# An mLSTM layer and a gated FFN in one kernel: the hand-written sequence of all steps laid anew

## Chip, core and metric

The kernel runs on one core of one Trainium2 chip. The metric is the device time of one execution in microseconds (us). Three timed executions of the kernel before took 588.6, 589.43 and 590.79 us; their median is 589.43 us. One further execution was profiled, and all rows below are from it.

## What is computed

The reference first runs an mLSTM over 4 batches, 8 heads and 768 steps with head size 40, all in float32: at each step a state matrix `C` and a vector `n` fade by a forget gate and take in a new key and value, and the query reads them. Then it runs a gated feed-forward network (FFN) over all 3072 tokens (320 features, 1536 hidden):

```python
C = f_stab * C + i_stab * outer(vt, kt)
n = f_stab * n + i_stab * kt
y[t] = sigmoid(o_gate[t]) * (C @ qt) / maximum(abs(n @ qt), 1)
...
gate = sigmoid(x @ w_gate)
val = x @ w_val
out = (gate * val) @ w_out
```

## The kernel before

**Tiling.** The sequence is cut into 6 chunks of 128 steps. A chunk `c` and a batch `b` make a *unit*, and the unit's number is 4c + b, so there are units 0 to 23, and units 8 to 23 are those of chunks 2 to 5. Within a unit the attention is done as masked matrix products; between chunks a state `cst` is carried for each batch. When the units of a chunk are done, their outputs (`xh`, `xl`: two float32r parts of each number, since the FFN multiplies in three passes for accuracy) go through the FFN in *tiles* numbered 0 to 102. A full tile is 512 tokens wide, a half tile 256; half tiles are 0 to 7, 16 to 45 (chunk 1 and the first of chunk 2) and 79 to 102 (chunk 5).

**The order.** Every piece of work is put into a table under a short key, and a string `ORDER` says in which sequence the pieces are issued. A word is a key, `*3` repeats it, and `/` flips which of two PSUM banks (`pa0`, `pa1`) the next attention tile takes. Each engine and each queue runs its own pieces in the sequence of the string and waits only where data or a buffer isn't ready. Nothing else orders the work:

```python
for word in ORDER.split():
    if word == "/":
        other("pa")
        continue
    key, _, n = word.partition("*")
    for _ in range(int(n or 1)):
        f, args = todo[key].pop(0)
        f(*args)
```

**The keys.** For tile n: `tn` is one matmul of the 16 of the up projection (line 865), `pn` one matmul of the down projection (line 903; 12 in a full tile, 6 in a half one), and `tan`, `tgn`, `thn`, `tln` the gate's steps between them on ACT (ScalarE), DVE (VectorE) and POOL (GpSimd) (lines 878 to 892). Weights are decoded under `w...` keys. For unit n: `ln` with a letter loads q, k, v or o (line 310), `ldn` the decay matrix (line 409).

For units 8 to 23 the queries and keys are *turned* (heads and time exchanged) by a detour through a scratch array in device memory, where units of even batches share `scr0` and those of odd ones `scr1`:

- `an.0` and `an.1` turn 32x32 blocks of q and of k on DVE (line 603); `ahn.x` rounds to float32r on ACT or DVE (line 607); `aln.x` makes the low part on POOL (line 612).
- `asn.0` to `asn.3` save q, `asn.4` to `asn.7` save k, in strips of 32 partitions, on SP's DMA queue (line 616).
- `sn`, four times, loads the turned k (twice: `ks`) and then the turned q (twice: `qs`) for the scores (line 650). There is one buffer each of `ks` and `qs` for all units, so `sn` waits for the scores of unit n - 1.
- `aqn`, three times, loads the turned q again as `qk`, for reading the carried state (line 623). There are two buffers of it.
- `cin` multiplies the carried state by `qk` (matmul `in`, line 714): the first piece on PE (TensorE) that needs `aqn`. `bn.g` are the scores (line 693) and need `sn`.

Further keys of unit n that stand below: `cn` gathers the values (64 small matmuls, line 663), `zn` makes the chunk's contribution to the state (line 818), `dn` transposes the output for the FFN (line 783), `bmn.g` masks the scores on DVE (line 699), `ohn` and `on` halve and store a finished block of 128 output rows (lines 917 to 923).

```python
for x, i in ((1, 0), (0, 1)):
    put(f"s{n}", take, x, i, True)
    put(f"s{n}", take, x, i, False)
...
for j in range(3):
    put(f"aq{n}", keep, j)
```

The first two chunks (units 0 to 7) turn q and k by transposes on PE instead and have no such detour.

Of the kernel before, what the change touches and what calls it, by code (L numbers as in the profile page):

```python
# [144 lines left out]
p32 tg33 th33 p32 t34*3 p32 t34*2 p32 t34 b10.2 bm10.2 t34*2 p33 e12a t34*2 tl33 ci10 cf10 t34*2 p33 t34 p33 t34
p33 z10 e12 ta34 t34 tg34 t35*2 c10 cs10 th34 s11*4 aq11*3 cv10 p33 t35 ld13 t35*2 p33 t35 p34 tl34 t35*3 lv14 cg10
t35 zd10.1 t35*2 p34 lk13 cv10 t35 zm10.0 t35*3 p34 ct12 / ci11 bk11 ta35 tg35 p34*3 t36*2 th35 t36*3 tl35 t36
zd11.0 t36 v14 t36*9 p35*6 cv10 ta36 tg36 t37 th36 t37*7 zm10.1 t37 tl36 t37*6 ta37 cf11 t37 p36*3 za10.1 tg37
# [982 lines left out]
```

## Time and profile before

| | before |
|---|---|
| median of 3 runs | 589.43 us |
| the profiled execution | 588.31 us |
| its span (first to last instruction) | 586.5 us |
| PE busy / weight loads | 526.6 us (90%) / 469.9 us (80%) |
| DVE, ACT, POOL busy | 318.1, 211.9, 175.2 us |
| mean granted TensorE clock | 0.965 of full speed |
| moved by DMA | 75.55 MB |

A profile's page has the busy time of each engine, the chain of work that ended last, and groups of instructions by source line. Views of the trace give the waits of an engine and what ended each, the instructions in order of time, and busy times in chosen stretches. Times in rows count from the first instruction. "SPq" is the issue of a DMA by SP. A clock of 1.00 is 2.4 GHz, one of 0.50 is 1.2 GHz.

### The profile page before, as it was taken

To read this page: it belongs to the slowest core of one execution; us is meant where nothing else is said; L and a number is where in the kernel's file an instruction comes from. 1 tells how busy PE (TensorE), PEld (TensorE's weight loads), DVE (VectorE), ACT (ScalarE), POOL (GpSimd) and SP (SyncE) were. 2 spreads that over 40 slices of the span, in tenths; PEclk is the share of its full clock that TensorE was granted. 3 is DMA by queue.
4 is the path that set the end of the run, shared out by engine and by line. 5 is a ranking of instruction groups with operands and counts; after the bars stand their busy time and mean duration, and the time that the engine had idled before them with its cause. 6 is when DMAs were issued, how large, how long until landed. Compare 5 with 4: busy or idle time off the path is not lost.

```text
span 586.5 us, 12196 instructions
## 1 busy us (share of the span) xinstructions
PE 526.6 (90%) x4667; PEld 469.9 (80%) x4667; DVE 318.1 (54%) x740; ACT 211.9 (36%) x548; POOL 175.2 (30%) x251
## 2 busy tenths in 40 slices
PE   8889999998599989499997848999958999999997
PEld 7668878887599988488886737888847788899997
DVE  5999989785167456036553412655613446443332
ACT  5697576524025422043422313332222242122221
POOL 5544224646223314124232213434121211202100
PEclk9999999999799999799997978999987999999999
DMA  9987792426959856638594545978674756100000
GB/s 233 271 221 193 200 216 60 108 65 129 194 106 194 176 119 115 148 67 164 136 195 99 122 94 91 203 157 161 132 156 76 177 99 131 52 22 24 12 12 23
DMA packets 227578, 75.55 MB, mean 129 GB/s; under 512 B 207040, under 2 KB 215424, under 8 KB 227520
## 3 DMA queue, kind: packets, MB, share of 16 engines
q1 hardware_dynamic: 226432, 74.51, 59.2%
q8 instruction: 37, 0.61, 0.5%
q10 hardware_dynamic: 1088, 0.26, 0.2%
q14 instruction: 21, 0.17, 0.1%
HBM read 57.61 MB, written 17.14 MB: 127 GB/s over the span
## 4 chain that ended last, share of the span: by engine, by line
PE 65%; issue 11%; DMA 8%; DVE 7%; POOL 5%; SPq 3%; ACT 2%; DVEq 0%; POOLq 0%; ACTq 0%
PE pg L865 36%; PE po L903 17%; DMA qk<-scr0q 3%; SPq L616 2%; PE in L714 2%; PE av L663 2%; PE s L693 2%; DMA ks<-scr0k 1%; PE cs L818 1%; PE xt L783 1%; PE s L688 1%; POOL d L422 1%; PE mb L985 1%; DMA qk<-scr1q 1%; DMA d<-mscr 1%
## 5 line engine op out<-in xcount | busy, mean ns | idle before, releaser
L878 ACT ACTIVATE sg<-pg 128x256 f32<-128x256 f32 (+1 forms) x103 | 48.3, 469 | 235.3 <-PE pg L865 214.4
L881 DVE SCALAR_TENSOR_TENSOR sg<-sg,pg 128x256 f32<-128x256 f32 (+1 forms) x103 | 54.0, 524 | 130.1 <-ACT sg L878 109.4
L865 PE MATMUL pg<-xh,wh 128*128 128x256 f32 (+1 forms) x412 | 113.4, 344 | 2.6 <-ACT sg L878 1.5
L865 PE MATMUL pg<-xl,wh 128*128 128x256 f32 (+1 forms) x412 | 110.2, 335 | 0.0
L865 PE MATMUL pg<-xh,wl 128*128 128x256 f32 (+1 forms) x412 | 109.9, 334 | 0.0
L903 PE MATMUL po<-oh,gh 128*128 128x320 f32 x288 | 90.9, 321 | 4.9 <-DVE gh L888 2.5
L903 PE MATMUL po<-ol,gh 128*128 128x320 f32 x288 | 92.2, 323 | 0.0
L903 PE MATMUL po<-oh,gl 128*128 128x320 f32 x288 | 91.0, 323 | 0.5 <-POOL gl L892 0.4
L892 POOL TENSOR_TENSOR gl<-sg,gh 128x256 fp32r<-128x256 f32 (+1 forms) x45 | 44.1, 980 | 157.3 <-ACT gh L886 89.4
L865 PEld LDWEIGHTS pg<-xh,wh 128*128 128x128 f32 x412 | 71.7, 193 | 10.5 <-ACT sg L878 5.2
L865 PEld LDWEIGHTS pg<-xh,wl 128*128 128x128 f32 x412 | 71.4, 192 | 5.2
L865 PEld LDWEIGHTS pg<-xl,wh 128*128 128x128 f32 x412 | 70.6, 192 | 5.7
L903 PEld LDWEIGHTS po<-oh,gh 128*128 128x128 f32 x288 | 54.5, 191 | 9.7 <-ACT gh L886 3.8
L865 PE MATMUL pg<-xl,w 128*128 128x256 f32 (+1 forms) x206 | 60.2, 336 | 0.0
L903 PEld LDWEIGHTS po<-oh,gl 128*128 128x128 f32 x288 | 55.1, 192 | 4.2 <-POOL gl L892 0.8
L903 PEld LDWEIGHTS po<-ol,gh 128*128 128x128 f32 x288 | 55.0, 191 | 2.3
L714 PE MATMUL in<-cst,qk 120*128 120x123 f32 (+1 forms) x120 | 19.8, 310 | 40.2 <-DMA qk<-scr0q 33.3
L865 PE MATMUL pg<-xh,w 128*128 128x256 f32 (+1 forms) x206 | 53.7, 331 | 0.0
L714 PEld LDWEIGHTS in<-cst,qk 120*128 120x128 f32 (+1 forms) x120 | 18.7, 224 | 42.6 <-issue 42.0
L699 DVE TENSOR_TENSOR d<-s,d 128x384 f32<-128x384 f32 (+1 forms) x66 | 33.1, 508 | 34.1 <-PE s L693 31.6
L886 ACT ACTIVATE gh<-sg 128x256 fp32r<-128x256 f32 (+1 forms) x61 | 31.1, 510 | 39.9 <-DVE sg L881 34.7
L417 ACT ACTIVATE d<-d,at 128x128 f32<-128x128 f32 x136 | 43.0, 393 | 6.6 <-DMA d<-mscr 6.6
(170 smaller groups left out, 779.9 us busy)
## 6 DMA issues: line engine op xcount, KB each, us to landing
d<-mscr SPq DMA_DIRECT2D x22, 512.0 KB
k<-in_k_dram SPq DMA_DIRECT2D x24, 160.0 KB
v<-in_v_dram SPq DMA_DIRECT2D x24, 160.0 KB
o<-in_o_gate_dram SPq DMA_DIRECT2D x24, 160.0 KB
st_o<-in_moe_w_out_dram SPq DMA_DIRECT2D x12, 320.0 KB
out_dram<-ob SPq DMA_DIRECT2D x24, 160.0 KB
scr0q<-qt SPq DMA_DIRECT2D x32, 120.0 KB
scr1q<-qt SPq DMA_DIRECT2D x32, 120.0 KB
```

Of the source, the lines that this page charges most:

```text
L417: nc.scalar.activation(d[:, h, :], d[:, h, :], AF.Exp, bias=at[:, c, b * H + h : b * H + h + 1], scale=-1.0)
L616: nc.sync.dma_start(dst.rearrange("(g c) r -> c g r", c=32), both[x][32 * i : 32 * i + 32].rearrange("c x (j r) -> c (x j) r", r=32).bitca ...
L663: nc.tensor.matmul(dst[xs], lhs[:, xs], rhs, start=True, stop=True)
L693: nc.tensor.matmul(ps[g][:, m, :], ks[: 3 * D, h0 + m, :], qs[: 3 * D, h0 + m, :], start=True, stop=True)
L699: nc.vector.tensor_tensor(x, ps[g][:, :nh, :], x, ALU.mult)
L714: nc.tensor.matmul(pi[:, h0 : h0 + nh, :], qk[u][:r, g, :], cst[:r, b, g, : nh * DA], start=True, stop=True)
L865: nc.tensor.matmul(pg[x], w[:, a, fs] if a < 2 else w[:, fs], y[c][:, a, n0:n1], start=first, stop=a == 2 and y is xl)
L878: nc.scalar.activation(sg[0], pg[0], AF.Tanh, scale=0.5)
L881: nc.vector.scalar_tensor_tensor(sg[0], sg[0], 1.0, pg[1], ALU.add, ALU.mult)
L886: nc.scalar.activation(gh[u][:, :nt], sg[0], AF.Copy)
L892: E('gl0' if c == 0 else 'gl', f'tl{n}').tensor_tensor(gl[u][:, :nt], sg[0], gh[u][:, :nt].bitcast(F32), ALU.subtract)
L903: nc.tensor.matmul(po[t], g[c, j, t0][:, (t - t0) * P : (t - t0 + 1) * P], o[:, j, :], start=j == 0 and first, stop=j == NF - 1 and last)
```

## The change

Only the string `ORDER` differs. Old and new string hold the same 4513 pieces; `/` stands 21 times in the old one and 36 times in the new one. So no instruction, size, engine or buffer differs, and each engine, SP's queue and POOL's included, runs the same pieces in another sequence. The old string issues the turning of a unit in blocks (`as8.0` to `as8.7` in one run, then `s8`, then `aq8`); the new one deals its pieces out singly, among those of other units. The cut shows the places of units 8, 16 and 20 in the old string, and of 8, 18 and 20 in the new one:

```diff
     'EU': 8,
 ORDER = """
...
-bm7.2 cv6 ta16 tg16 cr6 cx6 lk9 ci7 cf7 zd7.1 p15 c7 cs7 z7 e9a zm7.0 p15 oh0 o0 a8.0 a8.1 t17*3 zm7.1 t17 cv7
-t17*2 ah8.0 ah8.1 th16 tl16 t17 al8.0 al8.1 t17*4 cg7 p15 t17*2 as8.0 as8.1 as8.2 as8.3 as8.4 as8.5 as8.6 as8.7 cv7
-p15*3 t17 oh1 p16*2 t17 lo9 p15 e9 p15*2 p16*3 t17 za7.1 d6 ta17 tg17 p15*2 v8 dx6 ct8 t18*3 th17 p16 t18*2 zd7.0
-tl17 oh3 t18*5 dy6 t18*6 ta18 tg18 th18 tl18 ld10 a9.0 a9.1 p17*3 t19 lv9 e9m t19 s8 ah9.0 ah9.1 t19*2 za7.0 t19*2
-p17 cv7 cr7 p17 s8*3 aq8*3 p17 al9.0 al9.1 o1 t19*9 p18*2 t19 p18*3 lk10 ta19 bd9 t20 tg19 t20*5 o3 th19 t20*4 tl19
-t20*3 p19 t20*3 p19 p18 p19 ta20 tg20 p19 e8 p19 as9.0 as9.1 as9.2 as9.3 as9.4 as9.5 as9.6 as9.7 t21 th20 t21 tl20
-ci8 t21 p19 p20*2 t21*7 lv10 t21 e10a t21*4 bk9 v10 ta21 p20 e8m p20 t21 tg21 th21 tl21 p20*2 bd8 t22 cf8 t22*2
...
-as16.5 as16.6 as16.7 t55*4 bd16 t55*6 p54*3 ta55 p54 tg55 p54 oh9 oh10 th55 o9 ct17 p54 tl55 t56*7 o10 p54 t56*3
-ld18 t56 s16 t56*3 s16 p55 t56 s16 aq16*3 ci16 ta56 cf16 a17.0 a17.1 t56 tg56 p55*5 th56 tl56 t57*3 p55 t57*3 p56
...
-/ ci18 zd18.1 bd19 bm18.1 t64 zd18.0 p62 cf18 p62 t64*2 b18.2 bm18.2 p63*3 p62 ta64 tg64 th64 lv20 s19*4 aq19*3 t65
-z18 zm18.0 za18.0 tl64 p63*7 bk19 t65*4 p64 zm18.1 t65 p64 e20m t65 c18 cs18 v20 lv21 cv18 za18.1 t65 lq22 t65 ld21
-cg18 lk21 t65*4 v21 cv18*2 cr18 t65*2 ci19 cx18 p64 ta65 p64 t65 t66 cf19 t66 p64*2 tg65 t66 b19.0 bm19.0 p63
...
+a8.0 p12 t14 p12 / a6.1 ta14 a9.1 a6.2 lq9 p12 t14 ah6.2 p12 lq10 ah6.1 t15 tg14 e6a t15 p13 t15 p12*2 t15*2 w28a
...
+p13*2 t15 dx5 t15 al8.0 t15 aq6.2 t15 tl14 p13 t15 aq6.1 t15 as8.2 a9.0 t15*2 as8.3 p14 / b6.2 dy5 as8.0 t15 bm6.2
...
+cv6*2 zm6.0 zm6.1 lk8 ah9.0 p14 za6.0 lq11 t16 bm7.0 t16 p14 t16 b7.2 cv6 oh0 ta16 e9a b7.1 ct7 bm7.2 o0 as8.1 t17
+t16 bm7.1 ci7 lv9 tg16 t17 p15 cf7 t17 zd7.1 th16 t17*3 a8.1 t17 tl16 t17 z7 ah8.1 t17*3 e9 t17 al8.1 c7 cr6 t17
+as8.6 cs7 t17 p15 aq8 p15 cv7 p15 cx6 cg7 t17 as8.4 p15*2 ta17 cv7*2 p15 as8.5 p16 ah9.1 t17 as8.7 p15*2 tg17 p16
+al9.1 ld10 / d6 th17 t18*2 oh1 p16 tl17 t18*2 oh3 t18 o1 t18*3 aq8 al9.0 t18*8 p16 ta18 p16 s8 p17*2 tg18 p17 aq8
+t19 th18 p16 t19 as9.2 cr7 t19*2 tl18 t19 dx6 t19 as9.7 t19*4 s8 t19 e10a t19*2 s8 t19*2 p17 s8 p18 ta19 p18 as9.0
...
+e9m t22 as10.1 tl21 t22*2 p21 t22*2 p21 t22 bd9 t22*2 p21 v8 ta22 bk9 / b8.1 ci8 aq9 tg22 bm8.1 as10.2 p21*2 t23
...
+p59 t61 s18 p60 t61 lo19 p59 t61 lv19 t61*2 c17 aq18 ta61 aq18 s18 p59 cs17 p59 s18 t62 cv17 t62 cv17 a20.0 t62*2
...
+p60 e18m t62 as19.4 cx17 tl61 t62 as19.5 t62*2 zd17.1 as19.7 ah19.0 d17 p60 ta62 p60 al19.0 p60*2 dx17 p60 t62 p61
+al20.0 dy17 p61 as19.3 p61 p60 tg62 p60 t63 lq21 v19 bd18 t63 zm17.0 t63 th62 aq18 t63 zm17.1 za17.0 t63 as19.0
...
+t63 p61 t64 tg63 t64*2 p61 / b18.1 ci18 bm18.1 p61 p62 cf18 p61*2 e20 b18.0 th63 t64 bm18.0 tl63 b18.2 t64 bm18.2
...
+za17.1 t64*2 p62*2 ta64 ld21 p63*2 z18 as20.3 e20a p62 as20.0 zm18.0 t65 p63 zm18.1 t64 lk20 p63*2 tg64 p63 as20.2
...
+zd18.0 t65*2 as20.1 p64 za18.1 p64 ta65 p64 cx18 t65 lo21 p64*2 tg65 b19.0 ci19 th65 p64 t66 cf19 t66*2 bm19.0
...
+p65*3 a20.1 p65 p66*2 t67*2 zm19.1 ah20.1 a21.0 t67*2 al20.1 p65 p66 za19.1 ah21.0 t67 a21.1 t67*2 al21.0 as20.5
+t67 ah21.1 t67 aq20 t67 oh12 as20.6 v21 t67 v20 zd19.0 t67 as20.4 t67 e20m t67 aq20 t67 o12 t67 ta67 p66 as20.7
+p66*2 al21.1 aq20 p66*2 tg67 p66 lk23 p66 t68 oh14 th67 t68 lk22 t68 tl67 t68 as21.7 t68*2 o14 t68 oh13 t68*2 o13
+t68*2 as21.2 p67 t68*2 s20 t68 s20 t68 p67 s20 t68 ta68 p66*2 s20 p67 ci20 tg68 as21.1 p67 zm19.0 t69 oh15 th68 t69
...
 """
 GROUPS = ((0, 3), (3, 3), (6, 2))
```

## Rows read from the trace of the kernel before

**Rows 1.** The page: busy time of each engine

```profile
PE 526.6 (90%) x4667; PEld 469.9 (80%) x4667; DVE 318.1 (54%) x740; ACT 211.9 (36%) x548; POOL 175.2 (30%) x251
```

**Rows 2.** Waits of PE: total us, times, longest us

```profile
PE in L714 <- DMA qk<-scr0q: 33.3, 4, 8.8
PE in L714 <- DMA qk<-scr1q: 6.9, 3, 4.4
...
PE s L693 <- issue: 2.1, 1, 2.1
```

**Rows 3.** Timeline of PE where the longest waits end [idle before <-releaser]

```profile
153.14 0.55 PE L714 MATMUL in<-cst,qk 120*128 120x123 f32 x1 [8.19 <-DMA qk<-scr0q]
...
245.45 0.55 PE L714 MATMUL in<-cst,qk 120*128 120x123 f32 x1 [8.35 <-DMA qk<-scr0q]
...
312.79 0.55 PE L714 MATMUL in<-cst,qk 120*128 120x123 f32 x1 [4.36 <-DMA qk<-scr1q]
...
344.82 0.55 PE L714 MATMUL in<-cst,qk 120*128 120x123 f32 x1 [7.94 <-DMA qk<-scr0q]
...
441.86 0.55 PE L714 MATMUL in<-cst,qk 120*128 120x123 f32 x1 [8.78 <-DMA qk<-scr0q]
```

**Rows 4.** Six stretches behind waits: length, busy PE, PEld, DVE, ACT, POOL, PEclk, DMA share, GB/s

```profile
153.14:157.02 3.88, 3.88 (x17) 3.88 (x18) 0.00 (x0) 0.00 (x0) 0.00 (x0) 0.50 1.08 178
...
441.86:447.15 5.29, 5.29 (x16) 4.52 (x17) 3.30 (x6) 0.00 (x0) 0.00 (x0) 0.50 0.31 57
sum 24.32, PE 24.31 PEld 22.68 DVE 10.60 ACT 0.00 POOL 4.67; mean PE 4.05 PEld 3.78 DVE 1.77 ACT 0.00 POOL 0.78
```

**Rows 5.** SP's timeline at unit 16, then the timeline's SP rows at unit 20

```profile
334.50 0.98 SPq L923 DMA_DIRECT2D out_dram<-ob  x2
...
336.15 0.74 SPq L650 DMA_DIRECT2D ks<-scr0k  x2
336.93 0.31 SPq L650 DMA_DIRECT2D qs<-scr0q  x1
337.28 1.34 SPq L623 DMA_DIRECT2D qk<-scr0q  x3
...
435.16 0.97 SPq L650 DMA_DIRECT2D ks<-scr0k  x2
436.18 1.12 SPq L623 DMA_DIRECT2D qk<-scr0q  x3
```

**Rows 6.** The chain in order of time: DMAs from issue to landing (start, us)

```profile
146.35 6.66 DMA qk<-scr0q
...
232.04 2.26 DMA scr0k<-kt
...
238.93 6.39 DMA qk<-scr0q
...
406.92 5.19 DMA qk<-scr1q
...
436.95 4.78 DMA qk<-scr0q
```

**Rows 7.** The same chain: runs of matmuls without a wait

```profile
82.02 1.17 PE po L903 x8
...
183.35 0.75 PE av L663 x64
...
392.11 3.74 PE pg L865 x16
...
528.82 1.80 PE pg L865 x15
```

**Rows 8.** Three longer stretches, columns as in rows 4

```profile
24.00:66.00 42.00, 37.62 (x370) 31.93 (x369) 40.86 (x112) 33.10 (x98) 14.93 (x21) 1.00 0.82 220
141.00:450.00 309.00, 261.18 (x2280) 233.78 (x2280) 142.52 (x318) 86.98 (x225) 91.52 (x127) 0.93 0.70 140
158.50:225.00 66.50, 63.51 (x730) 61.43 (x729) 40.56 (x103) 22.44 (x64) 18.25 (x27) 1.00 0.71 141
```

**Rows 9.** The page: DMA packets

```profile
DMA packets 227578, 75.55 MB, mean 129 GB/s; under 512 B 207040, under 2 KB 215424, under 8 KB 227520
```

More of the change, by code (lines that the diff above doesn't have):

```diff
@@ L145 @@
[L145 to L148, printed above, removed]
-zd10.0 p36*2 t38 th37 cr10 t38*3 v12 t38 tl37 cx10 b11.1 bm11.1 t38 p36 t38*7 za10.0 t38*3 ta38 e12m b11.0 p37*2
@@ L170 @@
-lk17 cg14 s15*2 aq15*3 ld17 cv14*2 cr14 cx14 t53*3 bd15 bk15 tl52 e16a p51*9 t53 lo17 lv17 t53*7 d14 ci15 ta53 p52
-p51 za14.1 cf15 p52 dx14 dy14 p52 t54*2 e16 p52 t54 p52*2 zd15.1 tg53 th53 t54*2 p52*2 t54*4 / b15.0 p52 tl53
-bm15.0 t54*2 ct16 lq18 t54 zd15.0 p52 t54*2 b15.1 bm15.1 p52*2 t54 b15.2 ta54 bm15.2 t54 tg54 c15 p53 th54 z15 cs15
-cv15 e17a zm15.1 p53 cg15 zm15.0 p53*3 cv15 p53*2 lk18 e16m a16.0 a16.1 cv15 ah16.0 ah16.1 p53 cr15 p53*2 za15.1
-p53 tl54 cx15 d15 dx15 lo18 p53 al16.0 al16.1 v17 p54*5 dy15 t55 oh8 o8 t55*5 as16.0 as16.1 as16.2 as16.3 as16.4
@@ L185 @@
-tg61 th61 b17.2 p60*2 t62 s18 p59 bm17.2 t62 tl61 s18 p60 t62 c17 lq20 t62 s18*2 aq18*3 cs17 cg17 z17 za16.0 t62*2
-zm17.1 cv17*2 lq21 cv17 t62 a19.0 a19.1 ah19.0 ah19.1 t62 p60 al19.0 al19.1 t62*2 p60 t62*2 cr17 p60*4 t62 p60 lo20
-t62 ta62 cx17 tg62 d17 dx17 dy17 p61*2 t63*4 zm17.0 t63 th62 t63 e19 t63 tl62 t63 ld20 t63*4 e19m as19.0 as19.1
-as19.2 as19.3 as19.4 as19.5 as19.6 as19.7 t63*4 ta63 p61 p62 tg63 p62 lk20 p61*2 p62 t64 zd17.0 za17.0 t64 e20a
-ct19 p61 p62*2 p61 t64 / b18.1 p61*3 t64 p61 th63 t64*5 p62 p61 p62 b18.0 t64*2 bm18.0 tl63 p62*2 za17.1 e20 t64*2
@@ new lines @@
+t36 a12.1 t36 bk11 t36*2 ci11 cg10 ah12.1 v12 t36*2 cv10 t36 cr10 t36 al12.1 t36 p35 ta36 p35*2 ct11 p35 tg36 p35
+cx10 p35 as12.4 zd10.1 cf11 t37*2 bk12 t37 ld13 t37 zd11.0 t37*2 as12.1 th36 t37*2 tl36 t37*3 as12.0 t37*4 as12.5
+t37 p36 ta37 p36 as12.6 / b11.1 zm10.1 tg37 lq14 p36 t38*2 th37 t38*2 p36 t38 tl37 t38*5 b11.2 t38*2 bm11.2 e13a
+t38*3 bm11.1 p37 p36 ta38 p36 / b11.0 t38 t39 bm11.0 t39*2 aq12 t39*2 tg38 p37 aq12 z11 th38 tl38 lo13 t39*6 c11
+t39 cs11 t39 lv15 t39*2 p37 cg11 p38 ta39 as12.7 p37 cv11 p38 e13 za10.0 p38 lv12 t39 t40*2 tg39 t40 ld14 t40*2 p37
@@ new lines @@
+aq12 p37 t40 th39 t40*2 cv11 t40 tl39 t40 p38 t40*3 p38 t40*2 / d10 s12 ta40 p39*2 dx10 t40 p39 p38 tg40 t41*3 cv11
+zm11.0 p39 th40 t41 cr11 t41 oh6 dy10 t41*4 tl40 t41 lo14 p39 t41*4 cx11 lk14 t41 zd11.1 p40*2 ta41 t41 s12 p40*2
+tg41 p40 s12 t42 za11.0 p39 t42 s12 t42 th41 oh7 t42*2 za10.1 t42 a13.1 tl41 t42 o7 / d11 t42*2 dx11 t42*3 p41 dy11
+t42*3 p40 zm11.1 p41 ta42 t42 za11.1 p41*2 tg42 p41 t43 a13.0 t43 th42 t43*5 tl42 t43 ah13.0 t43*3 ct13 t43*2
+al13.0 t43*2 p41 p42 ta43 p42 t43 e14a / ci12 as13.1 tg43 th43 p42 as13.0 t44*2 tl43 t44*2 e14 p42 o6 t44*8 ah13.1
@@ new lines @@
+s15 p51*2 s15 t53 th52 p51 lo17 / c14 t53 cs14 ld17 t53*2 cv14 cg14 p52 t53 cv14 p50 cv14 a16.0 p51 cr14 p51 t53*2
+tl52 p51 ah16.0 p51*2 t53 zd14.0 al16.0 t53 cx14 t53*3 za14.0 as16.1 t53 ta53 p51*2 as16.2 p52 p51 p52 tg53 d14 p52
+th53 t54 dx14 t54 ah16.1 t54 dy14 t54 e16 p51 al16.1 zd14.1 p52 za14.1 t54*3 e17a b15.1 as16.5 ci15 as16.4 as16.6
+p52 t54 cf15 as16.7 t54*2 bm15.1 lo16 t54 e16m / b15.0 tl53 as16.0 t54*2 bm15.0 as16.3 t54*2 zd15.1 p52 b15.2 ta54
+t54 bm15.2 c15 e17 tg54 p53 cs15 p53*3 cv15 p53 cv15*2 p52 cg15 p52*3 cr15 p52 z15 th54 cx15 p53*2 tl54 lk18 p53
@@ new lines @@
+as17.7 p55 zm16.0 p55 tg57 as17.6 p56*3 as18.5 p56 ct18 p56 as17.2 t58*2 p56 as17.5 p56 t58 as17.1 ci16 as18.4 t58
+zd16.0 cf16 t58*2 th57 e17m t58*5 tl57 t58*2 p57*2 t58*2 b16.1 ta58 b16.0 bm16.1 t58 ct16 p57*2 e18a tg58 p57 t59*2
+bm16.0 t59*3 b16.2 t59 bm16.2 s17 t59 p56 zd16.1 s17 p56 t59 za16.1 th58 o11 t59 a18.0 t59 s17 t59 s17 c16 tl58
+ah18.0 aq17 as18.7 al18.0 p58 cs16 aq17 p58 t59 cv16 t59 bd17 p57 as18.2 t59*2 p57*2 ta59 t59 aq17 p57 as18.0 p57
+p58 tg59 p58*2 t60 cv16 t60 as18.3 t60 p58 p57*2 p58 th59 t60 lq19 t60 cv16 za16.0 t60 as18.1 tl59 t60*3 lk19 cg16
@@ new lines @@
+al20.0 dy17 p61 as19.3 p61 p60 tg62 p60 t63 lq21 v19 bd18 t63 zm17.0 t63 th62 aq18 t63 zm17.1 za17.0 t63 as19.0
+ct19 t63*2 e19 tl62 as19.6 t63*2 as19.1 t63*2 ld20 t63 e19m t63 as19.2 t63 p61 t63 lq22 p61*2 ta63 p61 p62*5 t64
+t63 p61 t64 tg63 t64*2 p61 / b18.1 ci18 bm18.1 p61 p62 cf18 p61*2 e20 b18.0 th63 t64 bm18.0 tl63 b18.2 t64 bm18.2
+s19 t64 p63 lq23 p62*3 zd18.1 t64 aq19 v18 t64 bk18 aq19 p63 t64 s19 t64 c18 aq19 s19*2 p63 cs18 t64 lo20 t64
+za17.1 t64*2 p62*2 ta64 ld21 p63*2 z18 as20.3 e20a p62 as20.0 zm18.0 t65 p63 zm18.1 t64 lk20 p63*2 tg64 p63 as20.2
@@ new lines @@
+t70*4 p69 t70*2 p68 b20.0 ta70 t70 bm20.0 p69 b20.1 tg70 p68 p69 p68 b20.2 za19.0 t71 s21 bm20.2 t71 p69 bm20.1 s21
+t71*2 s21 a22.1 t71 aq21 t71*2 s21 t71 ah22.1 aq21 / c20 th70 al22.1 as22.3 p69 cs20 ld23 t71 e21a p69 as22.0 cg20
+p69*2 p68 cv20 t71 cv20 a23.0 t71 as22.2 p69 t71 tl70 t71 ah23.0 t71 lv22 t71 cv20 a23.1 p69*2 ta71 as22.7 p70*3
+e21 p70*2 t71 p69 t72 tg71 e22a t72 e21m t72 cr20 t72*2 p70*2 th71 cx20 t72*3 tl71 t72*5 p71 al23.0 p70 t72 p71 t72
+e22m t72 as23.2 ta72 b21.0 ci21 aq22 ah23.1 bm21.0 as23.1 ct21 t73 tg72 al23.1 t73*2 as22.6 p70 cf21 p70 aq22 p70
@@ new lines @@
+th95 t96*2 tl95 t96*7 p94 t96*6 p95*2 ta96 t96 p94 p95 tg96 p95 t97*2 th96 t97*5 tl96 t97*9 p96 ta97 p96*2 p95 tg97
+p95 p96*2 th97 t98*4 tl97 t98*3 p97 t98*8 p97 p96 ta98 p97*2 t98 p97 t99 tg98 t99*2 p97 t99 th98 t99*4 tl98 t99*8
+p98 ta99 p98*3 tg99 p98 t100 th99 t100*2 tl99 t100*13 p98 ta100 p99*3 tg100 p99 t101 th100 t101*2 tl100 t101*13 p99
+ta101 p99 p100*2 tg101 t102*3 th101 t102*4 tl101 t102*8 p100 t102 ta102 p100 p101 p100 tg102 p100 p101 th102 p101*2
+tl102 p101 p102*3 p101 p102 oh22 p102*2 o22 oh23 o23
```

213 lines of the change are left out of this document (103 added, 110 removed).

## The prediction

> **What bounds the kernel now.** I read the page first, then PE's waits, then PE's timeline where they end, then SP's queue at those places. PE is busy 526.6 of 586.5 us, no other engine over 318.1 [rows 1]: PE is the bound, about 60 us of the span are its gaps, and the question is what ends them. PE's waits answer it: `in` waits for `qk` from scratch seven times, 33.3 + 6.9 = 40.2 us, and the scores once, 2.1 us [rows 2]. Five of the seven are long, 4.36 to 8.78 us [rows 3]. Counting the `in` groups of six matmuls along PE's timeline, these are `ci8`, `ci12`, `ci15`, `ci16` and `ci20`; the two short ones are `ci11` and `ci19`. Behind the long waits and the scores' wait PE runs for a while at a granted clock of 0.50, that is 1.2 GHz: six stretches of 24.32 us together, PE busy throughout [rows 4]. At 2.4 GHz their work would take half, so 12.2 us are lost there.
>
> SP's queue shows why `qk` is late. At unit 16 the three `qk` loads are issued at 337.28 us, behind two stores, two loads of `ks` and one of `qs`; at unit 20 at 436.18 us, behind `ks` [rows 5]. PE has nothing left ahead of `ci` by then.
>
> **A yardstick: lead.** I count PE's pieces that stand in the string between the third `aqn` and `cin`, and price them from runs without a wait: an up matmul 3.74/16 = 0.234 us in a full tile and 1.80/15 = 0.120 in a half one, a down matmul 1.17/8 = 0.146, a gather 0.75 [rows 7]; other attention pieces at 0.3 to 0.9, by estimate from their matmul counts. In the old string the leads are, from unit 8 on: 5.1, 6.2, 14.3, **2.4, 1.2**, 12.2, 10.7, **4.2, 0**, 10.2, 14.7, **6.1, 0.6**, 7.5, 19.3, 1.8 us. The seven units that waited (8 and those in bold: 11, 12, 15, 16, 19, 20) are all under 6.2; the nine others are at 6.2 or more, but for unit 23, which had 1.8 and didn't wait. So, with one exception in sixteen, the lead sorts waiters from others. It also agrees with the DMA itself: from issue to landing a `qk` load took 6.66, 6.39, 5.19 and 4.78 us [rows 6].
>
> **The change, part by part.** Same pieces, new sequence; every term is one of place.
>
> 1. *`qk` earlier.* By the same count the new leads are, from unit 8: 11.6, 6.6, 11.7, 10.0, 11.2, 7.7, 13.0, 14.4, 9.6, 8.0, **5.9**, 8.5, **5.1**, 9.4, 21.4, 16.4 us. (Unit 20: 16 up and 9 down matmuls, 16 x 0.234 + 9 x 0.146 = 5.06.) At a landing of 6.66 us, the largest in the rows, units 18 and 20 still wait 0.8 and 1.6, all others not: 2.4 us. At 4.78 none waits. I take 2.4, since two of four landings are near 6.66 [rows 6]. Removed: 40.2 - 2.4 = 37.8 us.
>
> In the rows, the load issued with `ks` and `qs` just before it landed in 6.39 and 6.66 us, the one with only `ks` before it in 4.78 [rows 5, 6]. The Trainium skill (DMA: Bandwidth & Descriptors, Queues, rings and completion order) says that descriptors on one ring of a DMA engine are consumed in ring order, so what stands ahead in the queue is paid for; by it, unit 20, whose three `aq` now go ahead of all four `s`, would see the shorter landing and wait 0 instead of 1.6 us, and the sum would be 537. The trace agrees in direction.
>
> 2. *The clock.* All six half-speed stretches follow a wait of 2.1 us or more [rows 2 to 4]; with no wait left over 1.6 us, I take all 12.2 us as gained. If the residues keep two of them, 4 us come back; that is in the range.
>
> 3. *The scores.* One wait of 2.1 us [rows 2], at unit 16, whose lead from the last `s` to the first score was 5.7 us, the old string's smallest; in the new one the smallest is 6.6 (unit 13), and unit 16 has 10.2. Old leads of 5.9 and 6.5 (units 23, 17) didn't wait. Gain 2.1.
>
> 4. *The saves.* They start sooner: from `al16.0` to `ci16` the old string has 9.2 us of PE work, the new one 30.0; for unit 20 it is 8.1 and 40.4. The issue of each `as`, about 0.55 us on SP, is paid in both. What is queued behind them: at units 13, 17 and 18 a strip of the next unit stands ahead of the third `aq` (`as19.3` before `aq18`), and it waits for that unit's `al` on POOL, which SP's other pieces behind then wait for too. The strips stand 8 us or more ahead of `ci` in PE work, against one 0.9 us instruction and a landing: no wait.
>
> 5. *The flips.* `a8.1` and `a23.1` now stand only 1.6 and 1.1 us of PE work behind a save of an earlier tile of the same three buffers; a save lands in 2.26 us [rows 6] after 0.55 of issue, so DVE could stand 1.2 + 1.7 = 2.9 us. It holds the gate's steps behind it, on which PE waits; but DVE is busy 40.56 of 66.5 us there [rows 8]. Between 0 and 2.9; nothing shows which, so I take the middle, 1.4.
>
> 6. *The opening* (to 66 us) is re-sequenced too. DVE is busy 40.86 of 42 us from 24 to 66, PE 37.62 [rows 8]; the work is the same, so PE could gain at most its 4.4 us of gaps and lose about as much if DVE's sequence is worse. I take 0.
>
> 7. *The gate steps and the last chunk.* Work between a tile's last up matmul and its first down matmul has a median of 2.9 us in the old string and 3.1 in the new; the words from tile 80 to 102 differ little. 0.
>
> **Sum.** 588.3 (the profiled execution) - 37.8 - 12.2 - 2.1 + 1.4 = 537.6. The median of the runs is 1.1 above the profiled one: 538.7, so **539 us**, about 8.6% less.
>
> **Rivals.**
>
> *Crowded transfers.* Unchanged DMA work must fit into less time: from 141 to 450 us the DMA engines are busy 0.70 of 309 us, 216 us; without 54 us of waiting that is 0.85 of the time [rows 8]. For it: 207040 of 227578 packets are under 512 B [rows 9], and the landing was longest where most was queued. Against: on the mean there is still room. If a landing takes 9 us, the new leads fall short at units 9, 13, 17, 18, 19 and 20 by 2.4 + 1.3 + 1.0 + 3.1 + 0.5 + 3.9 = 12.2 us; at 10 us by 19.2 with two half-speed stretches (4 us). That gives 549 to 560 us. The Trainium skill (DMA: Bandwidth & Descriptors, Specifications) wants 512 B or more a transfer for line rate, and most packets here are below it; by that rule the transfers would be the next bound, and this rival the outcome. The trace shows 140 GB/s at a share of 0.70 [rows 8], which goes with it, but no stretch in which `qk` alone waited on bandwidth.
>
> *Slower: the landing doubles.* The same mechanism pushed further: at 13.3 us, twice 6.66, thirteen of the sixteen leads fall short, by 54.6 us in all, nine of them by over 2.1, with 18 us of half clock: 533.8 + 54.6 + 18 + 1.1 = 607 us. It decides from a landing of about 12 us, where the same sum (39.7 + 16) brings back the old time. No `qk` landing in the rows is beyond 6.66.
>
> *The wait moves within SP's queue, no change.* The third `aq` of units 8, 13, 16, 17, 18, 19 and 20 stands behind something that itself waits (an `s` waiting for scores or saves, a store, a strip of the next unit). If five of these bring back what the five long waits cost, 40 + 12 us, it ends at 586 to 590. Against it: in those places the awaited piece stands 6.9 us or more of PE work ahead of `ci`.
>
> *The change does nothing.* Excluded as such: the string is all that orders the work, so the queue does differ.
>
> **How the numbers follow.** The measurement can tell about 0.5% (3 us) from no change. Forecast as above, 531 to 548: 0.66. Crowded, 549 to 563: 0.16. Below 531, the opening gaining too: 0.06. No change: 0.05. Slower: 0.07. The range takes the low end from the sum with neither residue nor flips (534.9) less the opening's 4.4, so 531, and the high end from the crowded case, 563. Faster is 0.66 + 0.16 + 0.06 = 0.88.
>
> **What would show it.** Right: `in` <- `qk` in PE's waits falls from 40 us to under 6; no clock of 0.50 between 141 and 450 us; PE busy little changed in us except for the 12 of half clock, its share up to some 95%. Term 1 is wrong if `in` still waits for `qk` at unit 18 or 20 by more than 2 us; term 5 if SP's saves end DVE's waits. The crowded rival shows as longer landings of `qk` and a DMA share near 0.85 with new waits. If PE's waits name the gate steps, the loss is in term 7.

## The result, and the profile after

The changed kernel takes **533.58 us** (median of four runs, 533.42 to 533.77) against 589.32 for the kernel before beside it: a ratio of 0.905, 95% interval [0.903, 0.907], 55.7 us less. The forecast was 539 us in a range of 531 to 563.

The page of the changed kernel, busy times and granted clock (tenths of full speed, 40 slices of the span):

```profile
span 531.6 us, 12197 instructions
...
PE 513.6 (97%) x4667; PEld 461.7 (87%) x4667; DVE 330.0 (62%) x740; ACT 211.1 (40%) x548; POOL 173.0 (33%) x251
...
PEclk9988999999999999999999999999999999999999
```

The same 4667 matmuls take 513.6 us instead of 526.6, and PE is idle for 531.6 - 513.6 = 18.0 us where it was 59.9 [rows 1]. DVE has the same 740 instructions as before and is busy 11.9 us longer; 5.4 us of that lie ahead of tile 8, of which the last section tells, and the rest is not looked into. The waits of PE from tile 8 to the end (line numbers are 16 higher than before):

```profile
PE po L919 <- DVE gl L908: 2.0, 2, 1.1
PE pt L585 <- DVE qk L596: 0.3, 1, 0.3
PE pg L881 <- ACT sg L894: 0.3, 1, 0.3
```

No `in` waits for `qk` any more (40.2 us before), and the scores wait 0.2 us where it was 2.1 [rows 2]. How much of the gain is waiting and how much is clock, and where some was lost, shows when the span is cut at the first matmul of tile 8. PE's windows up to there and from there on (length, busy PE, clock, DMA share, GB/s), first before, then after:

```profile
0.00:65.80 65.80, 58.27 (x593) 1.00 0.89 227
65.80:586.50 520.70, 468.31 (x4076) 0.96 0.56 116
```

```profile
0.00:71.60 71.60, 60.45 (x594) 0.95 0.79 197
71.60:531.60 460.00, 453.18 (x4076) 1.00 0.64 134
...
141.00:395.00 254.00, 252.59 (x2334) 1.00 0.82 169
```

From tile 8 on, the same 4076 matmuls end 60.7 us sooner: idle time falls from 52.4 to 6.8 us (45.6) and busy time from 468.3 to 453.2 (15.1), with the clock at 1.00 throughout. Ahead of tile 8 the new sequence **loses** 5.8 us.

### The profile page after: what moved, and what is told of

Its sections match the earlier page's. It is cut to its first block, busy times and chain, and to the rows that moved or that the text cites. A ratio compares the mean times of both kernels' runs of the same rounds, so it can differ in the third digit from the quotient of the medians.

```text
span 531.6 us, 12197 instructions
## 1 busy us (share of the span) xinstructions
PE 513.6 (97%) x4667; PEld 461.7 (87%) x4667; DVE 330.0 (62%) x740; ACT 211.1 (40%) x548; POOL 173.0 (33%) x251
## 4 chain that ended last, share of the span: by engine, by line
PE 77%; DVE 16%; issue 3%; POOL 2%; ACT 1%; DVEq 0%; POOLq 0%; ACTq 0%
PE pg L881 44%; PE po L919 21%; PE av L679 3%; PE s L709 2%; PE in L730 2%; DVE dc L491 2%; PE cs L834 2%; DVE dc L483 1%; DVE dc L487 1%; PE xt L799 1%; DVE sg L897 1%; PE s L704 1%; DVE o L773 1%; DVE wl L532 1%; DVE gl L908 1%
## 5 line engine op out<-in xcount | busy, mean ns | idle before, releaser
L881 PE MATMUL pg<-xh,wh 128*128 128x256 f32 (+1 forms) x412 | 109.7, 337 | 1.5 <-DVE sg L897 0.7
L908 POOL TENSOR_TENSOR gl<-sg,gh 128x256 fp32r<-128x256 f32 (+1 forms) x45 | 42.9, 954 | 163.7 <-ACT gh L902 48.5
L919 PE MATMUL po<-oh,gh 128*128 128x320 f32 x288 | 89.7, 319 | 0.0
L919 PE MATMUL po<-ol,gh 128*128 128x320 f32 x288 | 89.4, 316 | 0.0
L919 PE MATMUL po<-oh,gl 128*128 128x320 f32 x288 | 86.7, 315 | 2.0 <-DVE gl L908 2.0
L881 PEld LDWEIGHTS pg<-xh,wh 128*128 128x128 f32 x412 | 69.4, 189 | 6.7 <-ACT sg L894 1.1
L881 PE MATMUL pg<-xl,w 128*128 128x256 f32 (+1 forms) x206 | 63.0, 335 | 0.0
L919 PEld LDWEIGHTS po<-oh,gl 128*128 128x128 f32 x288 | 53.3, 189 | 6.1 <-DVE gl L908 2.9
L881 PEld LDWEIGHTS pg<-xl,w 128*128 128x128 f32 x206 | 37.3, 190 | 2.5
L908 DVE TENSOR_TENSOR gl<-sg,gh 128x256 fp32r<-128x256 f32 (+1 forms) x58 | 32.7, 564 | 8.4 <-ACT gh L902 5.9
```

The costliest lines, as they stand in the source:

```text
L881: nc.tensor.matmul(pg[x], w[:, a, fs] if a < 2 else w[:, fs], y[c][:, a, n0:n1], start=first, stop=a == 2 and y is xl)
L908: E('gl0' if c == 0 else 'gl', f'tl{n}').tensor_tensor(gl[u][:, :nt], sg[0], gh[u][:, :nt].bitcast(F32), ALU.subtract)
L919: nc.tensor.matmul(po[t], g[c, j, t0][:, (t - t0) * P : (t - t0 + 1) * P], o[:, j, :], start=j == 0 and first, stop=j == NF - 1 and last)
```

## The experiments

All are rearrangements of the string (run 5 adds matmuls; runs 9, 10 and 12 have one more `/`, beside `ci8`). A "place" is counted in matmuls `t` and `p` of the FFN that stand ahead. Times are medians; a gain is against runs of the kernel before on the same chip (587.7 to 589.6 us).

| | kernel | us | ratio, 95% interval |
|---|---|---|---|
| 1 | old, turning at its new places | 547.04 | 0.929 [0.923, 0.934] |
| 2 | new, turning at its old places | 568.71 | 0.965 [0.960, 0.970] |
| 3 | new, only `aq` at its old places | 545.45 | 0.927 [0.920, 0.934] |
| 4 | new, with the old opening | 528.17 | 0.896 [0.892, 0.901] |
| 5 | old, waits filled with matmuls | 585.11 | 0.989 [0.985, 0.994] |
| 6 | old, saves early | 586.80 | 0.995 [0.992, 0.998] |
| 7 | old, `aq` ahead of `s` | 557.81 | 0.945 [0.941, 0.948] |
| 8 | new, fillers later in the opening | 533.67 | 0.904 [0.901, 0.908] |
| 9 | old, `ci` of five units later | 566.21 | 0.965 [0.959, 0.972] |
| 10 | 7 and 9 together | 548.59 | 0.935 [0.929, 0.942] |
| 11 | old, `aq` behind the saves of q | 572.32 | 0.975 [0.969, 0.982] |
| 12 | 10, and q of unit 20 turned early | 540.98 | 0.920 [0.914, 0.927] |

### 1. The turning alone

The old string with `a`, `ah`, `al`, `as`, `s`, `aq`, `lq` and `lk` of units 8 to 23 at the places of the new one:

```diff
-... tl66 a20.0 a20.1 t67*2 ah20.0 ah20.1 al20.0 al20.1 ... as20.0 as20.1 as20.2 as20.3 as20.4 ... s20 aq20*3 ... ci20
+... a20.0 p59 t62*2 ... ah20.0 p60 ... as20.3 ta64 ... as20.0 z18 ... aq20 t67 as20.6 ... aq20 ... s20 t68 p66 ci20
```

> The old string, with only the turning of units 8 to 23 (loads of q and k, flips, rounding, low parts, saves, and the loads s and aq) set where the new string has it, by the count of t and p pieces before. Theory (the turning's place is the gain): the seven waits for qk and the half clock behind them go, 589.3 - 40.2 - 2.1 - 12.2 = 535, between 530 and 545 us. Rival (all engines' other pieces carry half or more of it): 560 us or more.

547.04 us, 42.3 less: three quarters of the 55.8, and 2 us above the range of the theory. What is left are short waits for `qk` and a new one. The waits of PE, then ACT's and PE's timelines at the new one, and SP's longest wait between 270 and 290 us:

```profile
PE pg L868 <- ACT sg L881: 8.7, 4, 6.6
PE in L717 <- DMA qk<-scr0q: 4.2, 2, 2.1
...
293.32 1.28 ACT L420 ACTIVATE d<-d,at 128x128 f32<-128x128 f32 x4 [11.39 <-DMA d<-mscr]
...
294.86 0.57 ACT L881 ACTIVATE sg<-pg 128x512 f32<-128x512 f32 x1
...
295.49 1.22 PE L868 MATMUL pg<-xh,wh 128*128 128x512 f32 x2 [6.62 <-ACT sg L881]
...
SPq L313 <- PE cs L821: 7.4, 1, 7.4
```

Line 881 here is the gate's step `ta`. It stands on ACT behind the exponentials of a decay matrix, whose load (`d<-mscr`) on SP's queue has become late, since turning pieces now stand ahead of it: SP stands 7.4 us, up to 280.7, at a load of k until PE has read the buffer's old content, and only then issues the saves and loads that stand before the decay matrix. Dealing one unit's pieces among others pushes what they overtake.

### 2. All but the turning

The reverse: the new string, the turning at its old places (and `bk12` behind `a12.1`, on which it depends).

```diff
-... a20.0 t62*2 ... ah20.0 ... aq20 ... aq20 ... s20 t68 s20 t68 p67 s20 ... s20 p67 ci20
+... t67 a20.0 a20.1 t67 p65 ah20.0 ... s20 t68 s20 aq20*3 p67 t68 ta68 p66 s20 ... s20 p66 p67 ci20
```

> The reverse: the new string with only those pieces set back to the old places (bk12 moved behind a12.1, which it must follow). Theory: the waits come back, 533.6 + 54.5 = 588, between 575 and 600 us, with in <- qk about 40 us in PE's waits. Rival: at most 560 us.

568.71 us: between the two ranges, 6 us below the theory's and 9 above the rival's. With the turning of before, the rest of the new string still gains 20.7 us, and its waits for `qk` are 17.5 us instead of 40.2. So the turning is not all. Counting places in the two strings shows what else moved: `ci`, the piece that waits, stands 40, 14, 14, 13 and 41 matmuls later in units 8, 11, 12, 15 and 16 (run 9 tests this).

### 3. Only `aq`

```diff
-... ah21.1 t67 aq20 t67 oh12 as20.6 ... e20m t67 aq20 ... al21.1 aq20 p66*2 ... s20 p67 ci20
+... s20 t68 s20 t68 aq20*3 p67 s20 t68 ta68 p66*2 s20 p67 ci20
```

> The new string with only the qk loads (aq of units 8 to 23) set back to the old places, saves early as in the new one. If a late issue of the loads is enough: by the leads of 5.1, 2.4, 1.2, 4.2, 0, 6.1, 0.6 us at units 8, 11, 12, 15, 16, 19, 20 and a landing of 4.8 to 6.7 us, 16 to 27 us of waits and up to 8 of half clock, 549 to 568 us. If it is the lateness of the saves that makes the wait, the loads find their data ready and the time stays at 534 to 540 us.

545.45 us, between the two. Of PE's waits for `qk` three came back, at `ci12`, `ci20` and `ci23`:

```profile
231.27 0.87 PE L725 MATMUL in<-cst,qk 120*128 120x123 f32 x6 [0.88 <-DMA qk<-scr0q]
...
396.38 1.54 PE L725 MATMUL in<-cst,qk 120*128 120x123 f32 x6 [5.95 <-DMA qk<-scr0q]
...
454.29 0.87 PE L725 MATMUL in<-cst,qk 120*128 120x123 f32 x6 [1.24 <-DMA qk<-scr1q]
```

My expectation took the leads of the old string, but `ci` stands later in the new one (run 2). Counted in the string that ran, the matmuls `t` and `p` between the third `aq` and `ci` are 5 at unit 20, 12 at unit 23, 23 at unit 12, and 31 or more at the thirteen others: the three units with the smallest lead are the three that waited. So the yardstick holds here.

Runs 2 and 3 have `aq` and `ci` at the same places and differ only in the rest of the turning. With that at its old places too, units 12, 16, 19 and 20 wait 8.4, 1.4, 0.5 and 7.2 us, and the kernel takes 23.3 us more. So it also counts how early the other pieces go; the pair does not separate the saves from `s`.

### 4. The old opening

The old string up to the first `t8`, then whatever is left in the order of the new one:

```diff
-... b4.1 ta7 w17b w16a w17b t7 w17b p6 t8 aq4.2 t8 w17f ...
+... b4.1 ta7 w15e p5 w18a b4.0 bm4.1 w17b v5 gs zd4.1 gs bk4 p6 t8*2 w17f ...
```

> The old string up to the first t8, then what is left in the new string's sequence. The changed kernel reached t8 at 71.6 us where the old one reached it at 65.8. If that loss is carried to the end: 533.6 - 5.8 = 528, between 525 and 531 us. Rival (the rest of the new sequence is paced by DVE or transfers, which catch up): 532 to 535 us.

528.17 us, 5.4 less than the changed kernel: the best of all. Its windows, cut at tile 8 as above:

```profile
0.00:66.00 66.00, 58.61 (x594) 1.00 0.88 229
66.00:526.70 460.70, 453.14 (x4075) 1.00 0.62 131
```

The two halves are those of the old opening (65.8) and of the new rest (460.0). So the loss lies in the opening alone.

### 5. The waits filled

The old string with 34, 35, 17, 33 and 36 dense matmuls of 128x128 ahead of `ci8`, `ci12`, `ci15`, `ci16`, `ci20`:

```diff
+    def fill(n, count):
+        pf = bank_tile([P, P], f"fill_{n}")
+        for _ in range(count):
+            nc.tensor.matmul(pf, ident, ident, start=True, stop=True)
...
-... aq20*3 t68*2 p66 ci20 ta68 ...
+... aq20*3 t68*2 p66 fi20 ci20 ta68 ...
```

> The string of before, with dense matmuls of a ready tile (155 of 128x128 in all) put just ahead of the five ci with the long waits, about as long as each wait. The loads are not touched, so the waits stay. Theory: the half-speed stretches come from PE standing still in these waits; filled, the clock stays at 1.00 there, and the kernel gains what the five stretches lost, some 10 us of 589: 576 to 582. Rival: the clock falls for another reason than the gaps: the stretches of 0.50 remain, 586 to 592.

585.11 us, 3.7 to 9.1 us less by the interval, below the forecast. The clock fell no more behind four of the five filled places. Behind the fifth the fill had ended 2.79 us too soon, and the clock fell; PE's timeline there:

```profile
340.81 3.51 PE L1092 MATMUL fill<-ident 128*128 128x128 f32 x30
...
347.11 1.46 PE L710 MATMUL in<-cst,qk 120*128 120x123 f32 x6 [2.79 <-DMA qk<-scr0q]
```

PE's work at half speed is 12.7 us here (5.9 after a wait of 3.1 us at unit 11, 3.4 each after this one and after the scores' 2.6), where it was 24.3 before. So 11.6 us of work are back at full speed, worth 5.8 us. This execution gained nothing from it: the fills and the waits left hold PE for 35.4 + 10.5 = 45.9 us at `in`, 5.7 more than the 40.2 of before. It was also the slowest of the five (588.88 us, mean clock 0.988); the four others took 583.25 to 585.21 us at 0.994 to 0.997. Unit 11's half speed is new: it had waited 1.5 us before, without a fall. A gap of PE does bring the half speed behind it; I had counted on more of the stretches to go, and not on the fills' own time.

### 6. Only the saves early

`a`, `ah`, `al`, `as`, `lq` and `lk` of units 8 to 23 at their new places in the old string; `s` and `aq` stay:

```diff
-... tl66 a20.0 a20.1 t67*2 ah20.0 ah20.1 al20.0 al20.1 ...
+... p59*4 a20.0 p59 t62*2 tg61 th61 b17.2 p60 ah20.0 p60 ...
```

> The string of before, with a, ah, al, as and the loads lq and lk of units 8 to 23 at the places that the new string gives them; s and aq stay where they were. Theory (late saves): in the old string the third aq is late because it stands behind saves that wait for al on POOL; with the saves early, most of the 42 us that the whole turning gained in the first run here comes at once: 545 to 558, waits of in for qk under 10 us. Rival (places of s and aq): the loads themselves stand too late, so the saves alone bring little: 572 to 590, waits of in for qk over 28 us. A time between would say that both matter.

586.80 us: the theory of the late saves falls as I had put it. The waits of PE are as long as before:

```profile
PE in L714 <- DMA qk<-scr0q: 29.2, 4, 8.9
PE in L714 <- DMA qk<-scr1q: 12.4, 3, 9.8
```

q of unit 20 is saved 28 us ahead of `ci20` here, 13 before, and yet its last `qk` load is issued 4.5 us ahead of `ci20` (before 4.9). SP's longest wait between 412 and 441 us:

```profile
SPq L616 <- POOL kt L612: 11.5, 1, 11.5
```

The first save of k waits 11.5 us for POOL's low part of k, and `s` and `aq` stand behind k's saves. So an early save of q is of no use here, with `aq` queued behind the saves of k.

### 7. Only `aq` ahead of `s`

```diff
-... ld18 t56 s16 t56*3 s16 p55 t56 s16 aq16*3 ci16 ...
+... ld18 t56 aq16*3 s16 t56*3 s16 p55 t56 s16 ci16 ...
```

> The string of before, with the three aq of a unit moved ahead of its first s; the saves stay. Theory (late saves): each aq goes out only as much earlier as the four s took to issue, 1.0 to 3.3 us at the five long waits, 10 us in all, and the scores may lose some of it: 575 to 586. Rival (the order in the queue): without ks and qs ahead of it a qk load also lands some 2 us sooner, and the long waits about halve: 560 to 574.

557.81 us, 31.8 less, more than either theory gave. One exchange of neighbours in SP's queue, at 15 units, is worth over half of the whole change. PE's waits, its timeline at units 8, 12, 16 and 20, then the chain at units 8 and 20 and SP's timeline at unit 16:

```profile
PE in L710 <- DMA qk<-scr0q: 15.0, 4, 5.6
...
149.20 1.31 PE L710 MATMUL in<-cst,qk 120*128 120x123 f32 x6 [4.42 <-DMA qk<-scr0q]
...
232.25 0.87 PE L710 MATMUL in<-cst,qk 120*128 120x123 f32 x6 [1.06 <-DMA qk<-scr0q]
...
319.14 0.87 PE L710 MATMUL in<-cst,qk 120*128 120x123 f32 x6 [3.90 <-DMA qk<-scr0q]
...
411.46 1.55 PE L710 MATMUL in<-cst,qk 120*128 120x123 f32 x6 [5.57 <-DMA qk<-scr0q]
...
143.42 5.53 DMA qk<-scr0q
...
408.94 2.28 DMA qk<-scr0q
...
314.38 1.18 SPq L619 DMA_DIRECT2D qk<-scr0q  x3
315.66 0.71 SPq L646 DMA_DIRECT2D ks<-scr0k  x2
```

Two things change, and at these four units each is worth half. The table counts from the moment when PE has nothing left ahead of `in` (us, before / run 7):

| unit | last `qk` load issued | from there to `in` |
|---|---|---|
| 8 | 1.4 / -1.4 | 6.8 / 5.8 |
| 12 | 1.8 / -2.3 | 6.5 / 3.4 |
| 16 | 1.3 / 0.0 | 6.7 / 3.9 |
| 20 | 3.9 / 3.1 | 4.9 / 2.5 |

First, `qk` goes out 9.0 us earlier in all, since it no longer stands behind `s`. That is mostly the time that SP takes to issue the four `s` and what stands among them; SP stood there 0.3 and 0.6 us for the landing of k's saves at units 8 and 12, and not at all at 16 and 20. At the units of `scr1` that waited (11, 15 and 19, 6.9 us in all, of which nothing is left) SP did stand at `s`, 3.0, 1.2 and 2.2 us, for the scores of the unit before. Second, `qk` lands sooner, 9.3 us in all, since no load of `ks` and `qs` lies ahead of it: unit 8 5.53 instead of 6.66 us, unit 20 2.28 instead of 4.78 [rows 6]. This is the rule that the prediction took from the Trainium skill (DMA: Bandwidth & Descriptors, Queues, rings and completion order), and these landings agree with it: the transfers ahead cost 1.1 and 2.5 us. So my theory had the one half and the rival the other.

With 25.2 us less of waits for `qk`, and PE's work at half speed down from 24.3 to 14.5 us (4.9 us), 30.1 of the 31.8 us are accounted for.

### 8. Fillers in the new opening

```diff
-... bd0 iq ex10 ... x3 iq qb11 ... qb10 iq ... cr0 iq ... cx0 iq ti10 ... g wre dx1 w3b t0 dy1 t0 w3d ...
+... bd0 ex10 ... x3 qb11 ... qb10 ... cr0 ... cx0 ti10 ... g wre dx1 w3b iq*4 t0 dy1 iq*4 t0 w3d ...
```

> The new string, with the last eight of the twelve warming matmuls (iq) moved to the first up tile, four ahead of it and four behind its first matmul, about where the old string has ten of them. The new opening loses about 6 us to the old one up to 66 us. Theory: half of that is the clock, 0.50 for 6.8 us behind gaps in which PE stands (3.4 us), the other half PE's gaps; the fillers save the first half-speed stretch: 531 to 533 against the 533.6 of the changed kernel. Rival: the clock falls all the same, or the fillers hold t0 up: 533 to 536.

533.67 us, the time of the changed kernel. In the profiled execution, 533.35 us, the clock stays at full speed from the start; in the three others its mean is 0.993, as in the changed kernel, and they take 533.54 to 534.27 us. So the fillers do not keep the clock up every time, and where they do, it brings under 1 us: the half speed in the opening costs next to nothing, because PE does not bound it. What does, stands in the last section.

### 9 and 10. `ci` later, alone and with `aq` first

```diff
-... s16 aq16*3 ci16 ta56 cf16 ...
+... s16 aq16*3 ta56 ... tl57 e17 t58 ci16 cf16 p56 ...
```

> The string of before, with ci of units 8, 11, 12, 15 and 16 (and cf, zd of the same unit, where they stood nearer to it) at the later places that the new string gives them: behind 40, 14, 14, 13 and 41 more matmuls t and p. Nothing of the turning moves. Theory: the lead between aq and ci is made as much by a later ci as by an earlier aq. 40 pieces are 8 us and cover the waits of units 8 and 16, 14 are 2.8 and cover unit 11 and a third of units 12 and 15; unit 20 stays. About 17 of 40 us of waits remain, and the clock behind the covered ones: 555 to 566. Rival: a later ci holds up the state and the output behind it, new waits of the gather or of the state take the place: over 570.

566.21 us, 21.5 less: at the upper end of the forecast, and about the gain of run 2 (20.7). `qk` waits are 18.8 us, in run 2 17.5. Run 2 also pays 6.5 us in its opening, up to tile 8; from there on its profiled execution is 26.5 us shorter than before and this one 24.1. So the later `ci` is most of what run 2 kept.

> Both edits in the string of before: the three aq ahead of the first s of their unit, and ci of units 8, 11, 12, 15 and 16 later as in the run beside it. Theory: of the waits that the first edit alone left (units 8 4.4, 12 1.1, 16 3.9, 20 5.6 us) only unit 20's stays, with one half-speed stretch: 542 to 548. Rival: the two edits remove the same waits and the rest is bound elsewhere: 553 to 558, as with the first alone.

548.59 us, 0.6 above the forecast. Together the two edits bring 39.1 us, not 31.8 + 21.5: they remove partly the same waits. What is left of PE's waits:

```profile
PE in L710 <- DMA qk<-scr0q: 6.0, 1, 6.0
...
PE s L689 <- DVE t L714: 2.6, 1, 2.6
PE s L689 <- DMA qs<-scr0q: 2.4, 1, 2.4
```

These are 11.0 us, and behind them PE works 10.1 us at half speed (5.0 us): the profiled 549.7 - 16.0 = 533.7, 5.2 above the profiled execution of run 4, the new rest with the old opening. Those 5.2 us I can't assign.

### 11. `aq` further ahead still

The three `aq` right behind the last save of q, ahead of the saves of k:

```diff
-... as20.2 as20.3 as20.4 as20.5 as20.6 as20.7 ... s20 t68 s20 aq20*3 t68*2 p66 ci20
+... as20.2 as20.3 aq20*3 as20.4 as20.5 as20.6 as20.7 ... s20 t68 s20 t68*2 p66 ci20
```

> The string of before, with the three aq of a unit right behind the save of its last strip of q, ahead of the saves of k. Theory: the turned q is held up in SP's queue by the turning of k, which ci does not need; without it aq goes out some 2.3 us behind the last q save, 2.4 to 4.2 us earlier than with aq ahead of s only, and 5 of that run's 15 us of waits remain: 540 to 549. Rival: SP stands still for the landing of the q saves, k's saves and all behind them come that much later, and scores or other loads wait instead: 553 to 565.

572.32 us, 15.4 less than before: the rival's course, and worse than it. The wait for `qk` all but goes (1.4 us), but others come. Waits of PE, waits in SP's queue, the chain, and ACT's timeline:

```profile
PE pg L861 <- ACT sg L874: 10.1, 5, 4.5
...
SPq L619 <- DMA scr0q<-qt: 19.4, 11, 3.4
SPq L619 <- DMA scr1q<-qt: 19.1, 8, 3.7
...
172.61 3.25 DMA scr0q<-qt
...
179.31 4.29 DMA d<-mscr
...
183.62 1.28 ACT L413 ACTIVATE d<-d,at 128x128 f32<-128x128 f32 x4 [5.88 <-DMA d<-mscr]
```

SP now stands 38.5 us in front of `aq` until q's own saves have landed, and all behind it comes later. The chain follows it: landing of the save, `aq`, k's saves, a decay matrix, the exponentials on ACT, and the gate's step behind these. As a place for `aq`, ahead of `s` is right; directly behind what it waits for itself is wrong.

### 12. Saves early, with `aq` free

Run 10, with q of unit 20 loaded, turned and saved at the new places, and `aq20` right ahead of k's saves:

```diff
-... ld22 lo22 as20.0 as20.1 as20.2 as20.3 as20.4 as20.5 as20.6 as20.7 ... aq20*3 s20 ...
+... a20.0 ... ah20.0 ... al20.0 ... as20.3 ... as20.0 ... ld22 lo22 aq20*3 as20.4 as20.5 as20.6 as20.7 ... s20 ...
```

> The string of the tenth run (aq ahead of s, ci of five units later), and for unit 20 alone the whole turning of q (lq20, a20.0, ah20.0, al20.0, as20.0 to as20.3) at the places of the new string, with the three aq20 right ahead of unit 20's saves of k. In the sixth run early saves brought nothing. Theory: they did not because aq stood behind s; where nothing that waits stands ahead of aq any more, an early save counts: unit 20's wait of 6.0 us goes, and the half-speed stretch of 6.8 us behind it (3.4 us): 536 to 542 against 548.6. Rival: the place of the saves doesn't matter and qk of unit 20 is late for another reason: 545 to 551.

540.98 us, 7.6 less than run 10 (which ran on another chip; against the kernel before beside each, 47.8 and 39.1, it is 8.7). Unit 20's wait of 6.0 us is gone, and so is the half speed behind it, 3.2 us of work or 1.6 us. SP's timeline, and its wait ahead of k's saves (385 to 392 us):

```profile
386.40 1.26 SPq L620 DMA_DIRECT2D qk<-scr0q  x3
390.80 2.51 SPq L613 DMA_DIRECT2D scr0k<-kt  x4
...
SPq L613 <- POOL kt L609: 3.1, 1, 3.1
```

The last `qk` load goes out 10.0 us before PE reaches `ci20`; in run 10 it went out 3.4 us after. `aq` now passes the place where SP stands for k's low part on POOL. Save and load were moved together here: that the early save was needed is not shown, since run 11, with q's saves at their old place, left only 1.4 us of unit 20's wait. With this the old string, changed in three ways, has 47.8 of the gain.

## Why the prediction was right, point by point

**Forecast.** 539 against 533.6: the mechanism was right, and the sizes erred in both directions. That they came so close is in part luck: with the old opening the new string takes 528.17 us (run 4), below the low end of the range.

1. *`qk` earlier.* Predicted -37.8, all but 2.4 of the 40.2 us. All 40.2 went: units 18 and 20 do not wait. Their last `qk` loads go out 6.1 and 4.4 us before PE reaches `ci`, near the leads of 5.9 and 5.1 by the string, so they landed within that; unit 20's within less than the 4.78 us of before, as the ring-order sentence had it. The lead was lengthened from one end by a later `ci` (21.5 us alone, run 9). The prediction counted this without naming it. But the yardstick takes SP to be on time, and in the old string it was late: moving `aq` ahead of `s` (31.8 us alone, run 7) adds only 0 to 16 matmuls to the leads of the seven units that waited, and 25.2 us of waits go. So the yardstick fits the changed kernel and run 3, not run 7; and it does not tell the time, since run 11 had longer leads than run 7 and lost to it by 14.5 us.
2. *The clock.* Predicted -12.2. No half speed is left from tile 8 on, and busy time of the same 4076 matmuls fell by 15.1. Run 5 bears out that the half speed follows the gaps; the 2.9 us more I can't assign.
3. *The scores.* -2.1, as predicted: 0.2 us is left.
4. *The saves.* Predicted 0. Alone they bring 2.8 us (run 6). In the new string the early turning other than `aq` is worth 23.3 us (runs 2 and 3), but no run separates the saves from `s` there.
5. *The flips.* Taken at +1.4; it is 0: the trace shows 0.1 us of idle time of DVE ahead of the 32 turning steps `a` together (line 619 after).
6. *The opening.* Taken at 0, bounded by 4.4 either way. This term was the largest miss: +5.8, outside its bound. The bound rested on "the work is the same", and the work on DVE is not the same length when it meets other work on POOL (below).
7. *Gate steps and last chunk.* Small waits of PE fell by a further 3.3 us (45.6 - 40.2 - 2.1), of which the prediction had none.

Against the profiled 588.3: the terms from tile 8 on were 50.7 us in the prediction and 60.7 on the chip; the opening took 5.8 of that back.

**Rivals.** *Crowded transfers*: the DMA share rose to 0.82 between 141 and 395 us, close to the 0.85 named, and PE stood only 1.4 of these 254 us. 169 GB/s moved with the same packets as before [rows 9], more than the 140 there [rows 8], so the rule on packet size (the Trainium skill, DMA: Bandwidth & Descriptors, Specifications) did not become the bound here. *The landing doubles*: no sign; at unit 20 the last load landed within 4.4 us, at unit 18 within 6.1. *The wait moves within SP's queue*: not in the changed kernel, but real; runs 1 and 11 show it as a late decay matrix that holds the gate.

## What to carry to other kernels

In an in-order queue, put a load that an engine will wait for ahead of loads that are needed later: what stands ahead of it costs its issue, its own waits, and time in the transfer (run 7). But do not put it directly behind the write it depends on, or the queue stands for the landing and everything behind pays (run 11). A distance between producer and consumer can be won at either end: moving the consumer later gave 21.5 us here, moving the load 31.8. Count it in time as well as in the string, since the queue can be late. And count a wait of PE with the half clock that follows it.
